# The opening of a delta-rule and MoE kernel: three written-out stages replaced by one order from a list scheduler inside the kernel

## The chip, the cores and the metric

One NeuronCore of a Trainium2 chip runs the whole program. The metric is the device time of one execution in microseconds; the median of the runs is quoted. Engines are named as in the profile: PE is TensorE's matmul, PEld its weight load, DVE is VectorE, ACT is ScalarE, POOL is GpSimd, SP is SyncE (here it only issues DMAs).

## What is computed

Three layers, one behind the other, on 4 x 768 = 3072 tokens:

```python
# 1: delta rule, 4 x 8 heads, 768 steps, head size 48
y_t = q_t @ state;  state += beta_t * outer(kn_t, v_t - kn_t @ state)    # kn = k / (|k| + 1e-6)
# 2: 384 -> 1024 -> 1024 -> 384, with a product of two projections
x = (((x @ w1) * (x @ w2)) @ w3) @ w_out
# 3: softmax-weighted hidden layer, layer norm, projection
h = x @ w_in;  solu = h * softmax(h)
out = ((solu - mean) / sqrt(var + 1e-6) * g_ln) @ w_out2
```

Layer 2's weights arrive as 8-byte floats and are converted in the kernel; w3 @ w_out is multiplied once, so that layer 2 needs w1, w2 and one product matrix.

## The kernel before

**The delta rule by chunks.** The 768 steps of each of the four batches are cut into chunks of 64. Chunks of two batches alternate, so the code handles *pairs* of chunks c, c+1. Eight chunks (four pairs) make a *set*; there are six sets. A set needs these steps:

- `load(i)`, `norm(i)`: four times per set, k and q are loaded by SP as 128 tokens and k is normalised (Square and Sqrt on ACT, four DVE operations). `norm` then issues four SP DMAs of 48 KB that copy the normalised k into the ring `kst` (lines 259 to 262).
- `prep_t(i)` (transposes on PE, copies into `KQ` and the ring `QA`) and `prep_g(i)` (products of keys and queries, four ACT copies, four masked DVE multiplications for each chunk).
- `invert(n)`, `invert_end(n)`: the triangular inverse of a whole set on DVE, 31 steps of two dependent operations (lines 342 and 348), two transposes before and after.
- `merge_1`, `merge_2`, `merge_3` for each pair: three rounds of small matmuls with copies in between, giving `TW`.
- `chain_u`, `chain_s`, `chain_y` for each pair, in sequence over all pairs: u from the state, the state's update, and the output y. y is written as two parts (`xb`) for layer 2.

**Layer 2** is `moe_block(j)`, twelve blocks of 256 tokens. A block is 14 portions: eight of 18 matmuls each (`pab`, line 591, with gate operations on ACT and DVE), then six of 12 (`px`, line 615). Its first reader of y is `pab`.

**The weights.** `weights_first` lists 18 pieces: four of w_out, eight of w3, three of w1, three of w2. `convert` turns a piece's 8-byte numbers into float32 in units of 384 or 512 columns: a low part (DVE, line 140), a high part (ACT Prelu, line 143), a shift (DVE, 150), an addition (DVE, 187). The w3 pieces are transposed on PE, copied on ACT (559), and multiplied with w_out (line 564); w1 and w2 are split into two parts (226 on ACT, 227 on DVE). The pieces of w_out and w3 are loaded by one DMA each, those of w1 and w2 by four for groups of 48, 48, 16 and 16 rows. They use seven slots, so a load waits until a slot's former piece has been used.

**The order of the work.** Before the main loop the program issues: four loads, set 0's `norm`, `prep_t`, `prep_g` with conversion steps put between them by `conv(x)` (a counter that lets some steps of the generator go), `invert(0)` with half a conversion step per operation, `invert_end(0)`. Then a loop over s = 0 to 23, a pair c = 2s each: `chain_u`, merges of the pairs to come, eight `turn`s, `chain_s`, `chain_y`. In the first two steps of a set the next set's `prep_t` and `prep_g` are done and its inverse is started; a `turn` also calls `fill(x)`, which lets x portions of layer 2 go. Block 0 may start when y of six chunks is there (`moe_all`, LAG = 2, line 759), and the conversion must be drained when c reaches 6 (line 802). PE's order is pinned to the program's order from line 796 on; the other engines' orders are the framework's.

Of the kernel before, what the change touches and what calls it, by code (L numbers as in the profile page):

```python
# [20 lines left out]
def kernel(  # L21
# [15 lines left out]
    nc = tc.nc  # L37
# [20 lines left out]
    CD = 6  # L58
    LAG = 2
# [3 lines left out]
    P0, C0 = 4, 24  # L63
    EX = 2.0
    F1 = (0.58, 0.6, 0.66, 0.66)
    LO = 2
    Z0, Z1 = 24, 44
# [66 lines left out]


# [99 lines left out]

    def load(i):
        b, s0 = chunk_at(chunk_of(i))
        for src, dst in ((k, kt_of(i)), (q, qt_of(i))):
            t = src[b].rearrange("(p e) s d -> s p e d", e=2)
            nc.sync.dma_start(  # L240
                out=dst.rearrange("t p (e x) -> t p e x", e=2)[:, :, :, 0:D], in_=t[s0:s0 + 128]
            )

    def norm(i):
        kt = kt_of(i).rearrange("t p (e x) -> t p e x", e=2)[:, :, :, 0:D]
        sq = small(NP * 2 * D).rearrange("t (p e d) -> t p e d", e=2, d=D)
        ss = pr.tile([128, NP, 2], F32, name="ss")
        rn = pr.tile([128, NP, 2, 1], F32, name="rn")
        nc.scalar.activation(out=sq, in_=kt, func=AF.Square)
        nc.vector.tensor_reduce(out=ss, in_=sq, axis=AX.X, op=ALU.add)  # L250
        nc.scalar.activation(out=ss, in_=ss, func=AF.Sqrt)
        nc.vector.tensor_scalar(out=ss, in0=ss, scalar1=1e-6, scalar2=None, op0=ALU.add)
        nc.vector.reciprocal(out=rn[:, :, :, 0], in_=ss)
        nc.vector.tensor_tensor(out=kt, in0=kt, in1=rn.to_broadcast([128, NP, 2, D]), op=ALU.mult)
        for cc in range(2):
            sl = (chunk_of(i) + 2 * cc) % RQ
            for h in range(2):
                o = 64 * (1 - h)
                nc.sync.dma_start(
                    out=kst[sl * 2 // RQ][64 * h:64 * h + 64, sl % (RQ // 2)],  # L260
                    in_=kt_of(i)[64 * cc:64 * cc + 64, :, o:o + D],
                )
# [4 lines left out]
    def prep_t(i):  # L267
        pk = ps_prep.tile([128, NP, 128], F32, tag="prep", name="pk")
        for p in range(NP):
            nc.tensor.transpose(pk[:, p, :], kt_of(i)[:, p, :], ident)  # L270
        nc.scalar.copy(out=KQ[0:KA, :, :, 1, :], in_=pk[0:KA].rearrange("r p (g t) -> r p g t", t=HC))
        pq = ps_prep.tile([128, NP, 128], F32, tag="prep", name="pq")
        for p in range(NP):
            nc.tensor.transpose(pq[:, p, :], qt_of(i)[:, p, :], ident)
        r = pq.rearrange("r p (c t) -> r c p t", c=2)
        (nc.vector.tensor_copy if i < SETC else nc.scalar.copy)(  # L276
            out=KQ[0:KA, :, :, 0, :], in_=pq[0:KA].rearrange("r p (g t) -> r p g t", t=HC)
        )
        sl = chunk_of(i) % RQ
        qa, sl = qa_of(sl)  # L280
        nc.scalar.copy(out=qa[0:64, sl:sl + 3:2, :, 1, :], in_=r[0:64])
        held[0] = nc.scalar.copy(out=qa[64:KA, sl:sl + 3:2, :, 0, :], in_=r[64:KA])
        if i < 2:
            load(i + 4)
        if i > 3 and i + 2 < NT128:
            load(i + 2)

    def prep_g(i):
        for cc in range(2):
            c = chunk_of(i) + 2 * cc  # L290
            (qa, sl), u0 = qa_of(c % RQ), c % SETC * NP
            pg = ps_prep.tile([128, NP, 128], F32, tag="prep", name="pg")
            for p in range(NP):
                for g in range(2):
                    for h in range(2):
                        r = slice(64 * (1 - h), 64 * (1 - h) + D)
                        o, x = 64 * h + HC * g, slice(HC * g, HC * g + 3 * HC)
                        nc.tensor.matmul(  # L298
                            pg[o:o + HC, p, x], KQ[r, p, 2 * cc + g, 1, :],
                            KQ[r, p, 2 * cc:2 * cc + 2].rearrange("r g k t -> r (g k t)")[:, x],  # L300
                            start=True, stop=True, skip_group_check=True,
                        )
            gd = GD[:, u0:u0 + NP, :]
            nc.scalar.copy(out=gd[:, :, :], in_=pg[:, :, HC:C])
            nc.scalar.copy(out=G21[:, c % SETC], in_=pg[:, :, HC:C])
            nc.scalar.copy(out=gd[32:64], in_=pg[32:64, :, 3 * HC:128])
            held[0] = nc.scalar.copy(out=gd[96:128], in_=pg[96:128, :, 3 * HC:128])  # L307
            for h in range(2):
                for r, x, o in (
                    (slice(64 * h, 64 * h + 64), slice(HC, C), C), (slice(64 * h, 64 * h + HC), slice(0, HC), 0),  # L310
                ):
                    nc.vector.tensor_tensor(  # L312
                        out=qa[r, sl, :, h, x], in0=pg[r, :, o:o + HC],
                        in1=mask[r, x].unsqueeze(1).to_broadcast([r.stop - r.start, NP, HC]), op=ALU.mult,
                    )

    bl = pr.tile([128, NSET, HC], F32, name="bl")

    def load_beta():
        for b in range(B):  # L320
            nc.sync.dma_start(
                out=bd.rearrange("(o k b) p e g i -> o b (p e) k (g i)", k=CPB, b=2)[b // 2, b % 2],
                in_=beta[b].rearrange("h (k x) -> h k x", k=CPB),
            )
        t = bd.rearrange("(n c) p e g i -> e g (c p) n i", c=SETC)
        for h in range(2):
            for g in range(2):
                r = 64 * h + 32 * g
                nc.sync.dma_start(out=bl[r:r + 32], in_=t[1 - h, g])

    def invert(n):
        nc.vector.transpose(out=Lz, in_=GD.rearrange("p u j -> p j u"))
        nc.gpsimd.memset(Tt, 0.0)
        nc.scalar.copy(out=Tt.rearrange("p i c -> p (i c)")[:, 0:HC * HC:HC + 1], in_=bl[:, n, :])  # L334
        yield nc.vector.scalar_tensor_tensor(
            out=Lz, in0=Lz, scalar=-1.0, in1=bl[:, n, :].unsqueeze(1).to_broadcast([128, HC, HC]),
            op0=ALU.mult, op1=ALU.mult,
        )
        for j in range(HC - 1):
            m = HC - 1 - j  # L340
            t = tmp[:, 0:m * (j + 1)].rearrange("p (i c) -> p i c", c=j + 1)
            yield nc.vector.tensor_tensor(  # L342
                out=t,
# [3 lines left out]
            )  # L347
            yield nc.vector.tensor_tensor(  # L348
                out=Tt[:, j + 1:HC, 0:j + 1], in0=Tt[:, j + 1:HC, 0:j + 1], in1=t, op=ALU.add
            )  # L350

    def invert_end(n):
        nc.vector.transpose(out=Dt.rearrange("p u i -> p i u"), in_=Tt)
        nc.vector.transpose(
            out=D1n.rearrange("p u c -> p c u"), in_=Tt.rearrange("p i c -> p c i")
        )

    def vcopy(c):  # L360
        return nc.vector.tensor_copy if 2 <= c < CA else nc.scalar.copy

    def dcopy(c):
        return nc.scalar.copy if c < 2 else nc.vector.tensor_copy

    def xcopy(c, lim):
        return nc.scalar.copy if c < lim or c % SETC >= SETC // 2 else nc.vector.tensor_copy
# [3 lines left out]
    def merge_1(c):  # L371

        tw, u0 = c % RT, c % SETC * NP
        both = slice(tw, tw + 2)
        mt = ps_prep.tile([128, 2, 2, NP, HC], F32, tag="prep", name="pm")
        pm, pt = mt[:, 0], mt[:, 1]
        for cc in range(2):
            for p in range(NP):
                for h in range(2):
                    nc.tensor.matmul(  # L380
                        pm[64 * h:64 * h + 32, cc, p, :],
                        G21[64 * h + 32:64 * h + 64, c % SETC + cc, p, :],
                        Dt[64 * h + 32:64 * h + 64, u0 + NP * cc + p, :],
                        start=True, stop=True, skip_group_check=True,
                    )
        xp = at.tile([128, 2, NP, HC], F32, name="xp")
        nc.scalar.copy(out=xp[0:32], in_=pm[0:32])
        vcopy(c)(out=xp[64:96], in_=pm[64:96])
        d = Dt[:, u0:u0 + 2 * NP, :].rearrange("r (c p) i -> r c p i", c=2)
        for g in range(4):  # L390
            r = slice(32 * g, 32 * g + 32)
            o = HC * (g % 2)
            (nc.scalar.copy if g < 2 else dcopy(c))(out=TW[r, both, :, g // 2, o:o + HC], in_=d[r])
        mg_t[c] = (xp, pt)

    def merge_2(c):
        xp, pt = mg_t.pop(c)
# [630 lines left out]
```

## Time and profile before

| | us |
|---|---|
| median of three runs (lowest, highest) | 863.81 (858.72, 864.83) |
| the profiled execution's own time | 862.37 |
| its span (first to last instruction) | 860.6 |
| PE busy | 802.0 (93%) |
| DVE busy | 581.9 (68%) |
| ACT busy | 467.7 (54%) |
| first `pab` matmul (layer 2 begins) | 153.72 |
| first `ph` matmul of the long last stage (layer 3) | about 633 |

Times in the rows count from the start of the span. A busy time is the union of an engine's instructions in a stretch, so overlapping instructions count once. The granted clock (PEclk) is given as a share of 2.4 GHz: 1.00 is that, 0.50 is 1.2 GHz.

### The profile page before, as it was taken

To read this page: it belongs to the slowest core of one execution; us is meant where nothing else is said; L and a number is where in the kernel's file an instruction comes from. 1 tells how busy PE (TensorE), PEld (TensorE's weight loads), DVE (VectorE), ACT (ScalarE), POOL (GpSimd) and SP (SyncE) were. 2 spreads that over 40 slices of the span, in tenths; PEclk is the share of its full clock that TensorE was granted. 3 is DMA by queue.
4 is the path that set the end of the run, shared out by engine and by line. 5 is a ranking of instruction groups with operands and counts; after the bars stand their busy time and mean duration, and the time that the engine had idled before them with its cause. 6 is when DMAs were issued, how large, how long until landed. Compare 5 with 4: busy or idle time off the path is not lost.

```text
span 860.6 us, 24611 instructions
## 1 busy us (share of the span) xinstructions
PE 802.0 (93%) x10256; PEld 731.3 (85%) x10256; DVE 581.9 (68%) x1522; ACT 467.7 (54%) x1127; POOL 46.2 (5%) x98
## 2 busy tenths in 40 slices
PE   4499668999999999999999999999999999999998
PEld 3366467999889999999999999999979999999997
DVE  4889996985497569756975596467656555555553
ACT  4564478457736764586468644565444443443442
POOL 7010000000000000000000000000001010000000
PEclk9999858999999999999999999999999999999999
DMA  9999814041413331332142113143331221221200
GB/s 225 299 235 155 130 20 82 15 94 30 95 30 66 78 68 36 82 69 61 35 85 48 43 35 95 30 125 107 119 122 58 72 64 56 74 65 56 74 28 28
DMA packets 140576, 70.74 MB, mean 82 GB/s; under 512 B 107057, under 2 KB 130865, under 8 KB 138673
## 3 DMA queue, kind: packets, MB, share of 16 engines
q1 hardware_dynamic: 138688, 57.64, 29.7%
q0 software_dynamic: 1776, 11.54, 4.2%
q8 instruction: 81, 1.33, 0.7%
q14 instruction: 31, 0.25, 0.1%
HBM read 47.91 MB, written 14.25 MB: 72 GB/s over the span
## 4 chain that ended last, share of the span: by engine, by line
PE 47%; issue 23%; DVE 16%; ACT 7%; DMA 3%; POOL 2%; SPq 0%; POOLq 0%; ACTq 0%; DVEq 0%
PE pab L591 17%; PE px L615 8%; PE pg L298 4%; DVE GT L348 3%; DVE tmp L342 3%; PE wps L564 3%; PE pw L425 3%; PE pu L451 2%; PE py L494 2%; PE pst L476 2%; DVE QA L312 2%; PE pm L404 2%; PE ph L918 1%; POOL vr L948 1%; DMA st_o<-in_moe_w_out_dram 1%
## 5 line engine op out<-in xcount | busy, mean ns | idle before, releaser
L591 PE MATMUL pab<-xb,w1s 128*128 128x256 f32 x864 | 123.7, 288 | 4.8 <-DVE asg L599 3.4
L591 PE MATMUL pab<-xb,w2s 128*128 128x256 f32 x864 | 119.2, 283 | 0.0
L591 PEld LDWEIGHTS pab<-xb,w1s 128*128 128x128 f32 x864 | 109.8, 191 | 8.7 <-DVE asg L599 4.7
L615 PE MATMUL px<-gh,Ws 128*128 128x256 f32 x864 | 112.7, 287 | 1.2 <-ACT gh L600 1.1
L591 PEld LDWEIGHTS pab<-xb,w2s 128*128 128x128 f32 x864 | 110.6, 192 | 0.0
L615 PEld LDWEIGHTS px<-gh,Ws 128*128 128x128 f32 x864 | 105.7, 191 | 3.3 <-ACT gh L600 1.5
L971 PE MATMUL po<-w4s,ln 128*128 128x384 f32 x432 | 79.8, 338 | 0.0
L918 PE MATMUL ph<-wis,x 128*128 128x512 f32 x288 | 76.7, 401 | 0.0
L600 ACT CAST gh<-asg 128x256 fp32r<-128x256 f32 x96 | 38.9, 405 | 68.6 <-DVE asg L599 67.6
L971 PEld LDWEIGHTS po<-w4s,ln 128*128 128x128 f32 x432 | 76.1, 188 | 0.0
L934 ACT ACTIVATE e<-ph,nm 128x1024 f32<-128x1024 f32 x24 | 26.8, 1118 | 87.5 <-DVE nm L933 86.0
L599 DVE TENSOR_TENSOR asg<-pab,asg 128x256 f32<-128x256 f32 x96 | 40.3, 420 | 46.4 <-ACT asg L598 46.1
L312 DVE TENSOR_TENSOR QA<-pg,mask 64x128 f32<-64x128 f32 x192 | 46.5, 281 | 34.2 <-ACT GT L307 19.4
L342 DVE TENSOR_TENSOR tmp<-D1n,GT 128x31 f32<-128x31 f32 (+15 forms) x186 | 63.0, 339 | 4.4 <-ACT GT L334 0.2
L348 DVE TENSOR_TENSOR GT<-GT,tmp 128x31 f32<-128x31 f32 (+15 forms) x186 | 63.1, 339 | 3.4
L918 PEld LDWEIGHTS ph<-wis,x 128*128 128x128 f32 x288 | 52.4, 189 | 10.6 <-issue 0.2
L598 ACT COPY asg<-pab 128x256 f32<-128x256 f32 x96 | 35.5, 370 | 40.9 <-PE pab L591 38.7
L933 DVE TENSOR_REDUCE nm<-ph 128x1 f32<-128x1024 f32 x24 | 29.4, 1225 | 40.4 <-PE ph L918 40.4
L298 PE MATMUL pg<-KQ 48*32 48x96 f32 x1536 | 44.0, 267 | 8.4 <-DVE KQ L276 7.7
L935 DVE SCALAR_TENSOR_TENSOR hs<-ph,e 128x1024 f32<-128x1024 f32 x24 | 29.4, 1225 | 30.9 <-ACT e L934 30.9
L601 DVE TENSOR_TENSOR gh<-asg,gh 128x256 fp32r<-128x256 f32 x96 | 40.4, 421 | 13.4 <-ACT gh L600 12.9
L298 PEld LDWEIGHTS pg<-KQ 48*32 48x32 f32 x1536 | 37.1, 118 | 13.1 <-ACT raw_w2s L143 6.3
(158 smaller groups left out, 1355.5 us busy)
## 6 DMA issues: line engine op xcount, KB each, us to landing
x2d<-xs SPq DMA_DIRECT2D x36, 256.0 KB, 2.4
x<-x2d SPq DMA_DIRECT2D x24, 384.0 KB, 3.6
X<-in_v_dram SPq DMA_DIRECT2D x48, 96.0 KB, 3.1
out_dram<-ot SPq DMA_DIRECT2D x24, 192.0 KB, 1.9
ktok<-in_k_dram SPq DMA_DIRECT2D x22, 192.0 KB, 3.8
qtok<-in_q_dram SPq DMA_DIRECT2D x22, 192.0 KB, 3.5
kst<-ktok SPq DMA_DIRECT2D x88, 48.0 KB, 2.9
raw_w2s<-in_moe_w_dram POOLq DMA_DIRECT2D x4, 1024.0 KB, 7.0
```

Of the source, the lines that this page charges most:

```text
L298: nc.tensor.matmul(pg[o:o + HC, p, x], KQ[r, p, 2 * cc + g, 1, :], KQ[r, p, 2 * cc:2 * cc + 2].rearrange("r g k t -> r (g k t)")[:, x], st ...
L312: nc.vector.tensor_tensor(out=qa[r, sl, :, h, x], in0=pg[r, :, o:o + HC], in1=mask[r, x].unsqueeze(1).to_broadcast([r.stop - r.start, NP, ...
L342: yield nc.vector.tensor_tensor(out=t, in0=Lz[:, j, j + 1:HC].unsqueeze(2).to_broadcast([128, m, j + 1]), in1=Tt[:, j, 0:j + 1].unsqueeze( ...
L348: yield nc.vector.tensor_tensor(out=Tt[:, j + 1:HC, 0:j + 1], in0=Tt[:, j + 1:HC, 0:j + 1], in1=t, op=ALU.add)
L591: nc.tensor.matmul(pab[:, e, :], ws[m][:, a, fs], xb[:, b, m, :], start=(n == 0), stop=(n == 3 * NM - 1), skip_group_check=True,)
L598: nc.scalar.copy(out=asb, in_=pab[:, 0, :])
L599: nc.vector.tensor_tensor(out=g, in0=pab[:, 1, :], in1=asb, op=ALU.mult)
L600: nc.scalar.copy(out=gh[:, 0, f, :], in_=g)
L601: gated[0] = nc.vector.tensor_tensor(out=gh[:, 1, f, :], in0=g, in1=gh[:, 0, f, :].bitcast(F32), op=ALU.subtract)
L615: nc.tensor.matmul(px, Ws[:, a, f, js], gh[:, b, f, :], start=(n == 0), stop=(n == 3 * NF - 1),)
L918: nc.tensor.matmul(ph[:, gs], x2[:, m, a, :], wis[m][:, b, gs], start=(n == 0), stop=(n == 3 * NM - 1),)
L971: nc.tensor.matmul(po, ln[:, a, f, :], w4s[f][:, b, :], start=(n == 0), stop=(n == 3 * NF - 1),)
```

## The change

Everything up to the end of set 0 (its four pairs' chain), all conversions, and set 1's `norm`, `prep_t`, `prep_g` and `invert(1)` are now one stretch, whose order on *every* engine is fixed by a list scheduler that runs while the program is built. Each step is a generator that yields operations with an engine, a cost in microseconds and a time from which its inputs are there; `Weave.go` picks, engine by engine, the earliest operation, and among those within `SLACK` the one with the lowest priority number. Costs, `TAIL` (time until another engine sees a result) and DMA landings (`land`) are constants. Some operations may go to either of ACT and DVE. `moe_block` runs in the same stretch as the thread of least priority. The main loop now begins with set 1 (s = 4).

```diff
-    CD = 6
-    LAG = 2
-    P0, C0 = 4, 24
-    EX = 2.0
-    Z0, Z1 = 24, 44
+    LW = 11
...
+    TAIL = {"PE": 0.21, "ACT": 0.13, "DVE": 0.12, "POOL": 0.15, "SP": 0.0}
+    SLACK = {"PE": 0.3, "ACT": 0.1, "DVE": 0.05, "POOL": 0.0, "SP": 0.0}
+    BIAS = {"PE": 0.0, "ACT": 0.0, "DVE": 0.3, "POOL": 0.0, "SP": 0.0}
...
+                        e, cost, fn = min(th[2][1], key=lambda a: max(self.free[a[0]], th[2][2]) + a[1] + BIAS[a[0]])
+                        best.setdefault(e, []).append((max(self.free[e], th[2][2]), th[0], th, cost, fn))
...
+                    first = min(x[0] for x in c)
+                    p = min((x for x in c if x[0] <= first + SLACK[e]), key=lambda x: (x[1], x[0]))
...
+    def store(i):
...
+                t = yield on("ACT", lambda e, sl=sl, h=h, o=o, cc=cc: plain(
+                    e, kst[sl * 2 // RQ][64 * h:64 * h + 64, sl % (RQ // 2)],
+                    kt_of(i)[64 * cc:64 * cc + 64, :, o:o + D]), 0.28, 0.28, t - 0.1)
...
+        t = yield op("PE", 0.46, lambda: turned(pk, kt_of(i)), at_)
...
+            t = yield op("PE", 0.75, products, ready.get(i, 0.0))
...
+    def unit(raw, o, n, at_, value, use):
...
+        a = yield either(
+            ("DVE", 0.08 + n / 1920, lambda: nc.vector.tensor_scalar(
+                out=low, in0=w[:, :, 0], scalar1=2.0 ** -29, scalar2=None, op0=ALU.mult)),
+            ("ACT", 0.06 + n / 1000, lambda: nc.scalar.mul(out=low, in_=w[:, :, 0], mul=2.0 ** -29)), at_)
...
+            "q0": lambda: ring[:, 0:2 * DFF], "q1": lambda: ring[:, 2 * DFF:4 * DFF],
...
+        "o0:a0 w0:b2 o1:a1 w1:q0 o2:b0 o3:b1 w2:q1 w3:xb w4:a0 w5:a1 w6:b0 w7:b1 "
+        "u0:q0 v0:q1 v1:b2 u1:a0 u2:a1 v2:xb"
...
+            if i == 0:
+                yield ("wait", came[3])
...
+                    todo_ = [(d[:, o:o + n], src[:, o:o + n]) for o, n in cuts(w)]
...
     def moe_block(j):
+        yield ("wait", ab_done)
+        yield ("wait", xb_set[j])
...
+    def first_chain():
...
+            if c == CPT:
+                yield ("wait", ab_done)
...
+            yield from chain_y(c, t)
...
+    def second_prep():
+        yield ("wait", inverted[0])
+        for i in range(SETC // 2, SETC):
+            yield ("spawn", 3.9, norm(i))
+        for x in ("u0", "v0"):
+            yield ("wait", spent[x])
...
+        for i in range(SETC // 2, SETC):
+            yield from prep_t(i)
...
+            yield from prep_g(i)
...
+        yield from beside(invert(1), 40, third_keys)
+        yield from invert_end(1)
...
+    for i in range(SETC // 2):
+        WV.spawn(0.1 + 0.01 * i, norm(i))
+        WV.spawn(0.2 + 0.01 * i, first_prep(i))
+    WV.spawn(0.3, first_inverse())
+    WV.spawn(0.3, first_merges())
+    WV.spawn(0.2, first_chain())
+    WV.spawn(4.0, convert_first(items))
+    WV.spawn(3.8, second_prep())
+    moe_thread = WV.spawn(9.0, mg, False)
+    WV.go()
...
-        chain_s(c)
-        chain_y(c)
-        y_done[0] = c + 2
+        run(chain_y(c))
+        run(chain_s(c))
```

Single conversion units are spawned with priority 5.0 and up. In the pieces' list `o`, `w`, `u`, `v` are w_out, w3, w1, w2, and the second name is the slot: `q0` and `q1` lie in the half of the `QA` ring that set 1 writes later (hence the wait for u0 and v0). A w_out or w3 piece is loaded by two DMAs of half its columns or rows. For sets 0 and 1 `store` replaces the `kst` DMAs by copies on ACT or DVE. Beta's first copy moves from SP's to ACT's queue, and SP's reload of it stands ahead of loads 2 and 3. `ab_done` is set when all 18 pieces are converted; block 0 waits for it. In the main loop y is done ahead of the state's update, and in a set's first two steps a `turn` lets the portion of layer 2 go before its other job.

## Rows read from the trace of the kernel before

**Rows 1.** Busy time of each engine by stretch, granted clock, DMA share, GB/s

```profile
core 0: us, PE busy (x) PEld busy (x) DVE busy (x) ACT busy (x) POOL busy (x), PEclk, DMA share, GB/s
0.00:153.00 153.00, 109.52 (x1418) 80.55 (x1420) 123.19 (x316) 92.56 (x217) 22.41 (x44) 0.89 0.78 162
7.00:153.00 146.00, 109.52 (x1418) 80.55 (x1420) 122.63 (x315) 90.22 (x214) 16.39 (x26) 0.88 0.77 163
0.00:10.00 10.00, 0.04 (x1) 0.07 (x2) 1.97 (x5) 3.82 (x5) 8.96 (x21) 1.00 0.99 185
70.00:80.00 10.00, 9.92 (x46) 6.58 (x45) 9.93 (x30) 4.95 (x10) 0.97 (x2) 1.00 0.89 136
110.00:120.00 10.00, 7.09 (x132) 6.15 (x132) 8.79 (x18) 8.77 (x22) 0.00 (x0) 0.50 0.10 19
158.70:190.00 31.30, 31.13 (x352) 30.34 (x353) 30.20 (x84) 14.75 (x38) 0.00 (x0) 1.00 0.23 46
190.00:240.00 50.00, 46.67 (x985) 43.38 (x984) 26.15 (x72) 35.49 (x98) 0.95 (x1) 1.00 0.31 68
```

**Rows 2.** PE in order of time: start us, us, engine, line, operation

```profile
10.84 1.06 PE L274 MATMUL pq<-ident,qtok 128*128 128x128 f32 x4
12.87 2.78 PE L298 MATMUL pg<-KQ 48*32 48x96 f32 x64 [0.97 <-DVE KQ L276]
...
134.34 0.63 PE L274 MATMUL pq<-ident,qtok 128*128 128x128 f32 x4 [0.84 <-DVE QA L312]
...
146.30 1.52 PE L298 MATMUL pg<-KQ 48*32 48x96 f32 x64
...
152.69 1.10 PE L425 MATMUL pw<-TW,kst 64*48 64x64 f32 x32
153.72 1.33 PE L591 MATMUL pab<-xb,w1s 128*128 128x256 f32 x9
```

**Rows 3.** DVE in order of time: inverse, end of conversion

```profile
100.74 1.90 DVE L353 STREAM_TRANSPOSE Dt<-GT 128x1024 f32<-128x1024 f32 x1
102.50 1.93 DVE L354 STREAM_TRANSPOSE D1n<-GT 128x1024 f32<-128x1024 f32 x1
...
126.14 0.69 DVE L227 TENSOR_TENSOR w2s<-raw_xb,w2s 128x512 fp32r<-128x512 f32 x1
```

**Rows 4.** Groups of instructions by line, engine, operation and tile

```profile
L348 DVE TENSOR_TENSOR GT<-GT,tmp 128x31 f32<-128x31 f32 (+15 forms) x186 | 63.1, 339 | 3.4
L342 DVE TENSOR_TENSOR tmp<-D1n,GT 128x31 f32<-128x31 f32 (+15 forms) x186 | 63.0, 339 | 4.4 <-ACT GT L334 0.2
L393 ACT COPY TW<-Dt 32x256 f32<-32x256 f32 x50 | 20.1, 403 | 17.3 <-DVE Dt L353 15.0 <-PE pu L451 1.8
L393 DVE COPY TW<-Dt 32x256 f32<-32x256 f32 x46 | 13.2, 287 | 3.1 <-PE pu L451 2.3
L140 DVE TENSOR_SCALAR t<-raw_w2s 128x512 uint32<-128x512 uint32 (+1 forms) x18 | 7.1, 406 | 0.1
```

**Rows 5.** DMA issues: queue, count, KB each, median us to landing

```profile
kst<-ktok SPq DMA_DIRECT2D x88, 48.0 KB, 2.9
raw_w2s<-in_moe_w_dram POOLq DMA_DIRECT2D x4, 1024.0 KB, 7.0
raw_w2s<-in_moe_w_dram SPq DMA_DIRECT2D x6, 384.0 KB, 5.6
stage_a<-in_moe_w_dram SPq DMA_DIRECT2D x2, 128.0 KB, 8.3
```

**Rows 6.** DMA issue on SP's and POOL's queues in order of time

```profile
98.14 1.52 SPq L178 DMA_DIRECT2D stage_a<-in_moe_w_dram  x3
...
12.21 0.92 POOL L178 DMA_DIRECT2D stage_a<-in_moe_w_out_dram  x1
```

More of the change, by code (lines that the diff above doesn't have):

```diff
@@ L253, in norm @@
[L253 to L257, printed above, removed]
-                o = 64 * (1 - h)
[L259 to L262, printed above, removed]
+        ss = pr.tile([128, NP, 2], F32, name="ss", bufs=2)
@@ L279, in prep_t, with queries @@
         sl = chunk_of(i) % RQ
         qa, sl = qa_of(sl)
[L281 to L284, printed above, removed]
+        def queries():
+            for o, x in ((qa[0:64, sl:sl + 3:2, :, 1, :], r[0:64]), (qa[64:KA, sl:sl + 3:2, :, 0, :], r[64:KA])):
+                e = yield on("ACT", lambda e, o=o, x=x: plain(e, o, x), 0.48, 0.6, b)
+            yield ("put", PP, e)
+            yield ("set", used[i], e)
@@ L285, in prep_t, with reload @@
+        yield ("spawn", 2.0, queries())
+        ready[i] = max(a, b)
+        def reload():
+            yield ("wait", stored[i])
+            yield from load(i + 2)
         if i > 3 and i + 2 < NT128:
-            load(i + 2)
+            yield ("spawn", 3.0, reload())
+    ready = {}
+    prepared = [Event() for _ in range(NT128)]
     def prep_g(i):
+        left, parts = [], []
         for cc in range(2):
@@ L354, in invert_end @@
[L354 to L367, printed above, removed]
+        yield op("DVE", 1.9, lambda: nc.vector.transpose(out=Dt.rearrange("p u i -> p i u"), in_=Tt))
@@ new lines, in use @@
+                t = yield op("PE", 0.46, turn, t)
+                yield ("set", turned_at[f"w{m}", o], t)
+                half_ = (o // 512) % 2
+                yield ("get", turned[half_])
+                w3t = bufs[half_][m % 2]
+                t = yield either(
+                    ("ACT", 0.48, lambda: nc.scalar.copy(out=w3t[:, 0:nb], in_=pt[:, 0:nb])),
+                    ("DVE", 0.6, lambda: nc.vector.tensor_copy(out=w3t[:, 0:nb], in_=pt[:, 0:nb])), t)
+                yield ("put", AB, t)
@@ new lines, in fill, with first_loads @@
+    def fill(x):
+        owed[0] = min(owed[0] + x, 3.0)
+        while owed[0] >= 1.0:
+            if not portion():
+                return
+            owed[0] -= 1.0
+    gated = [None]
+    head = tc.manual_schedule(engines=None)
+    head.__enter__()
+    warm = const.tile([128, 1], F32, name="warm")
+    nc.vector.memset(warm, 1.0)
+    nc.scalar.activation(out=warm, in_=warm, func=AF.Sqrt)
+    WV = Weave()
+    items = pieces()
+    def first_loads():
+        for i in (0, 1):
+            yield from load(i)
+        yield ("spawn", 4.0, fetch(items))
+        yield from load_beta_back()
+        for i in (2, 3):
+            yield from load(i)
+        for c in range(0, RX, 2):
+            yield from load_v(c)
+        yield op("SP", 0.6, lambda: nc.sync.dma_start(out=gl, in_=g_ln.rearrange("(k p) -> p k", p=128)))
+        for i in (4, 5):
+            yield ("wait", sent[NAMES[LW], 512])
+            yield ("wait", used[i - 4])
+            yield ("wait", stored[i - 4])
+            yield from load(i)
@@ L896 @@
     load_x2(1)
-    for x in mg:
+    while not over[0]:
+        portion()
         for _ in range(WO):
```

1041 lines of the change are left out of this document (717 added, 324 removed).

## The prediction

> **What bounds the kernel now.** I read the busy times by stretch first. From 158.7 us on PE is full (31.13 of 31.30 us), and in 190 to 240 it idles 3.3 us [rows 1]: layer 2 and the sets that follow are bound by PE. Ahead of that, no engine is full all the time: up to 153.0 DVE is busy 123.2 us, ACT 92.6 and PE 109.5, part of it at half clock (0.50 in 110 to 120) [rows 1]. Then PE in order of time: layer 2's first `pab` starts at 153.72, right behind a merge's `pw` [rows 2]. The work that PE has left at that moment fixes the end, since PE is full from there. So the question is when block 0 can start with the same work behind it.
>
> DVE in order of time tells why it is 153.72. Set 0's inverse ends with its two transposes at 100.74 and 102.50, and the last conversion (the split of w2's last unit) ends at 126.8 [rows 3]. From 104 to 153 the program issues merges, three pairs' chain and set 1's preparation in one written order, and in that stretch neither DVE nor ACT is full (8.79 and 8.77 of 10 in 110 to 120) [rows 1]. The early part is dense on DVE only (9.93 of 10 in 70 to 80, while ACT has 4.95) [rows 1]. So the stage is limited by DVE first and by latencies afterwards, and the two vector engines together have room: 215.8 us of work in 2 x 153.
>
> **The change part by part.**
>
> *Start of block 0.* In the changed code block 0 waits for y of the first two pairs and for `ab_done`, the conversion of all 18 pieces. Set 0's steps have the highest priorities, so its y is early; `ab_done` comes last, because single units have priority 5.0 and set 1's preparation 3.8. What must be done by then is nearly what the kernel before has done by 153: all conversions, sets 0 and 1 prepared, set 0's merges and most of its chain.
>
> *The sum of the two vector engines.* Before: 123.2 + 92.6 = 215.8 us [rows 1]. Added: `store` puts 2 sets x 4 x 4 = 32 copies on ACT or DVE in place of DMAs. The nearest rows are the copies of 32 x 256 elements, 0.287 us on DVE and 0.403 on ACT [rows 4], so 9.2 to 12.9 us; I take 11. (The DMA that goes took 2.9 us to land [rows 5]; it delays merges only, so I count nothing for its going.) Added also: that part of set 1's inverse that gets done ahead of the last unit. Its 62 operations take 0.339 us each, 21 us, with transposes some 26 [rows 4, 3]. They have the better priority, but an operation that depends on the one before is ready 0.12 - 0.03 = 0.09 us after that one's end in the scheduler's terms, beyond DVE's `SLACK` of 0.05; so where a unit's operation is ready it goes in between, and the two alternate. Once u0 and v0 are used, four pieces (8 units, 24 to 32 DVE operations) are left, and part of them go beside set 1's `prep`. I take 24 inverse operations ahead of the last unit, 8 us; the ends are 0 and 22. Sum 215.8 + 11 + 8 = 234.8.
>
> *How it is shared.* The low part (34 units, 0.406 us on DVE [rows 4]), the `KQ` copies, the transposed w3, `store` and the later halves of merges and chain may now go to either engine, and `BIAS` leans them to ACT. That is over 40 us that can be moved, more than the 31 us by which DVE led. So I take halves, 117.4 us each.
>
> *How full they get.* From 7.0, where norm(0) is about to finish, to 153 DVE was busy 122.6 of 146 us, 84% [rows 1]. In its dense stretch it was 99% [rows 1]. A fixed order made from constants will be worse than that and, with two chains of work and the conversions to choose from, better than 84%; I take 90%. Block 0 then starts at 7 + 117.4 / 0.90 = 137.4 us, 16.3 ahead of 153.72. The ends: 7 + (215.8 + 9.2) / 2 / 0.99 = 120.6 (33 us ahead), and 7 + (215.8 + 12.9 + 22) / 2 / 0.84 = 156.2 (2.5 late).
>
> *Work that moves behind block 0's start.* `chain_y(4)` waits for `ab_done` (its `xb` buffer holds w2's last piece), so one group of 32 matmuls, as long as the `pw` of 1.10 us [rows 2], moves behind: -1.1. What is left of inverse(1) runs beside `pab`, as it does before (DVE 30.20 of 31.30 with PE full [rows 1]): nothing. If that cover is gone, merges of set 1 are late, but two blocks' portions can fill PE there.
>
> *Queues.* SP: set 0's loads 2 and 3 now stand behind the reload of beta, which waits for beta's first copy; and POOL's weight loads wait for load 3, where the kernel before sent its second weight DMA at 12.21 and one from SP before that [rows 6]. I estimate weights 4 to 7 us later at the start, from nearby DMAs' landing times of 2.9 to 8.3 us [rows 5]. That hurts only while DVE waits for units in its first 20 us; it is in the 90%. At the other end nine slots stand in place of seven, so loads are issued earlier: before, the last ones were issued at 98.14 and landed 8.3 us later [rows 5, 6], far ahead of 137. Loads 4 to 7 of set 1 lie on SP behind waits for set 0's use of the buffers; who waits is set 1's norm, which has lower priority anyway.
>
> *Main loop.* y ahead of the state's update: the state's copies are read by the next pair's `chain_u`, four turns later, so I count 0. The swap inside a turn likewise. Both ends are 3 us, since all PE idles in 190 to 240 is 3.3 us [rows 1].
>
> Sum: 16.3 - 1.1 = 15.2 us. The profiled execution took 862.4 us (span 860.6 and 1.8 around it), 1.4 under the median of the runs; 862.4 - 15.2 = **847 us**.
>
> **The rivals.**
>
> *Better packing (832).* If units go first in practice and inverse(1) falls wholly behind, and the engines are nearly full, block 0 starts at 122. For it: DVE did hold 99% in a dense stretch. Against: set 0's preparation is a sequence of short dependent steps, and in 0 to 10 DVE has 1.97 us of work [rows 1].
>
> *Nothing gained (862).* All of inverse(1) gets ahead of the last units and the engines stay at 84%: block 0 at 154 to 156. The conversions before were done at 126.8; the change puts 26 us of set 1's inverse and its preparation in front of the last ones. What the early set 1 is worth would then be nothing, since PE was full beside inverse(1) already. Against it: the alternation worked out above.
>
> *Slower: PE's prices (881).* The scheduler prices four transposes at 0.46 us and a chunk's products at 0.75. Rows show 0.63 and 1.52 for two chunks at full clock, but 1.06 and 2.78 early on [rows 2], and a clock of 0.50 in 110 to 120 [rows 1]. Every engine's order is written as if results came at the cheap price. A DVE or ACT that has to wait for a late product holds back the conversion units queued behind it, though they are ready. Price: each `prep` is late by 2 x (1.06 - 0.46) + (2.78 - 1.50) = 2.5 us, eight of them 20 us; merges and chain of set 0, some 24 groups of matmuls at half clock, an estimated 0.6 each, 14 more. All 34 exposed would put block 0 at 171.4, and the end at 881. It is slower by over 1% once 24 of the 34 are exposed. Against: set 0's four `prep`s are late before as well, and then one or two engines wait at a time, with the other thread's work already queued ahead.
>
> *Halved weight loads (862).* A load of 1024 KB took 7.0 us to land, one of 384 KB 5.6, one of 128 KB 8.3 [rows 5]: time to land does not shrink with size. The change cuts 12 pieces into 24 DMAs. If two halves land one after the other, a piece takes about 11 in place of 7 us; over the eight w3 pieces 34 us, which moves the last landing from 106 to 140 and `ab_done` to about 153. In favour of it stands a rule; against it that both halves are issued at once and may overlap, and that a unit now waits for its half alone. The Trainium skill (DMA: Bandwidth & Descriptors, Rules for kernel authors) advises 128 partitions and at least 1 MiB for one DMA; by its fixed cost of about 2 us a DMA, 12 more would be an estimated 24 us if nothing overlapped. By that rule the change costs, by the rows it need not.
>
> **How the numbers follow.** Forecast 0.55 (its own range 838 to 858), better packing 0.13, nothing gained 0.17, halved loads 0.03, PE's prices 0.12. A measurement here tells about 1%, 8.6 us. Of the forecast's share 0.06 lies above 855. Faster: 0.49 + 0.13 = 0.62. Within 1%: 0.06 + 0.17 + 0.03 = 0.26. Slower: 0.12. The range reaches from 829 (a little beyond better packing, the low end's 33 us being 829) to 868, where part of the slow case is left out.
>
> **What would show it.** Right: first `pab` at 130 to 145; DVE and ACT busy shares in 20 to 130 both near 90%; low-part operations on ACT; about a third of inverse(1)'s operations ahead of the last split of w2; first `ph` earlier by as much as the first `pab`. Wrong: the last split of w2 near 150 with inverse(1) finished (nothing gained); DVE or ACT idle behind PE products with units queued (PE's prices); DVE idle behind weight DMAs beyond 40 us (halved loads); or a first `pab` that is early while PE idles afterwards by more than the 3.3 us of 190 to 240, in which case the gain is given back in the main loop.

## The result, and the profile after

| us | before | after |
|---|---|---|
| median (lowest, highest), four runs each | 862.31 (858.72, 864.83) | 848.05 (845.62, 848.62) |
| profiled execution, its span | 862.37, 860.6 | 848.23, 846.5 |
| block 0 of layer 2 runs without gaps from | 153.72 | 139.66 |
| `invert(1)`'s first closing transpose begins | 183.97 | 173.12 |
| first merge of set 1 (`pm`) | 187.24 | 175.30 |
| portions of layer 2 done by then | 15 | 16 |
| first `ph` (last stage) | 633.05 | 617.76 |

The ratio is 0.9839, with an interval of 0.982 to 0.9858: faster by 1.6%, 14 us. The forecast was 847.

Two rows of the kernel before belong to this table, the closing transpose on DVE and set 1's first merge on PE (columns of [rows 2]):

```profile
183.97 2.07 DVE L353 STREAM_TRANSPOSE Dt<-GT 128x1024 f32<-128x1024 f32 x1
187.24 0.69 PE L380 MATMUL pm<-Dt,G 32*32 32x32 f32 x32
```

Busy times by stretch of the changed kernel (us in the stretch, then busy us and instructions of PE, PEld, DVE, ACT and POOL, granted clock, DMA share, GB/s), in the columns of [rows 1]:

```profile
core 0: us, PE busy (x) PEld busy (x) DVE busy (x) ACT busy (x) POOL busy (x), PEclk, DMA share, GB/s
7.00:139.60 132.60, 101.54 (x1480) 71.45 (x1480) 110.93 (x303) 114.58 (x261) 24.73 (x42) 0.94 0.67 169
132.00:139.60 7.60, 2.64 (x42) 1.98 (x38) 7.53 (x17) 4.62 (x12) 0.96 (x1) 0.92 0.30 61
139.60:176.00 36.40, 35.83 (x349) 35.23 (x349) 33.64 (x96) 14.43 (x35) 0.00 (x0) 0.92 0.24 59
190.00:240.00 50.00, 48.54 (x1003) 45.56 (x1000) 34.54 (x101) 34.73 (x97) 0.96 (x1) 1.00 0.28 64
140.00:150.00 10.00, 10.00 (x111) 9.62 (x110) 8.31 (x25) 4.93 (x12) 0.00 (x0) 0.74 0.17 34
240.00:600.00 360.00, 352.71 (x5891) 339.02 (x5891) 245.24 (x674) 214.17 (x564) 3.69 (x5) 1.00 0.26 68
...
90.00:132.00 42.00, 36.58 (x925) 28.91 (x924) 30.84 (x88) 40.28 (x103) 2.30 (x2) 1.00 0.27 52
```

The work is now spread: in place of 122.6 us on DVE and 90.2 on ACT [rows 1], 110.9 and 114.6 us in 132.6, 84% and 86% full. Late in the stretch ACT is the fullest engine (40.28 of 42.00 in 90 to 132). From 139.60 on PE is full, as it was from 153.72.

PE in order of time of the changed kernel (start, us, engine, line, operation, idle time before and what ended it), in the columns of [rows 2]. Line 897 is w3 times w_out, 1023 is `pab`, 1065 `px`, 602 the first merge:

```profile
123.50 1.46 PE L897 MATMUL wps<-area,w3x 128*128 128x384 f32 x4
...
132.91 0.62 PE L1023 MATMUL pab<-xb,w1s 128*128 128x256 f32 x3
133.72 0.50 PE L1023 MATMUL pab<-xb,w1s 128*128 128x256 f32 x2 [0.20 <-ACT w1s L829]
136.78 0.61 PE L1023 MATMUL pab<-xb,w1s 128*128 128x256 f32 x3 [2.56 <-DVE w1s L830]
139.66 0.58 PE L1023 MATMUL pab<-xb,w1s 128*128 128x256 f32 x1 [2.26 <-DVE w1s L830]
140.04 2.12 PE L1023 MATMUL pab<-xb,w2s 128*128 128x256 f32 x9
...
147.66 1.24 PE L1023 MATMUL pab<-xb,w2s 128*128 128x256 f32 x9
...
175.30 0.69 PE L602 MATMUL pm<-Dt,G 32*32 32x32 f32 x32 [0.51 <-DVE Dt L558]
```

The first `pab` stands at 132.91, but it goes in small pieces until 139.66: it waits for the last splits of w1. Nine matmuls then take 2.12 us in place of 1.24. In 132 to 139.6 PE had been busy 2.64 of 7.60 us. In 140 to 150 the granted clock is 0.74, a mean of its levels 1.2 and 2.4 GHz: from 139.6 to 145 it is 0.50. The last line is the one that counts later: set 1's first merge waits 0.51 us for `invert(1)`'s transpose.

ACT in order of time (same columns) shows why those splits were late:

```profile
132.09 0.53 ACT L572 COPY GT<-pg 32x128 f32<-32x128 f32 x2
132.64 0.52 ACT L369 ACTIVATE t<-ktok 128x384 f32<-128x384 f32 x1
133.07 1.64 ACT L829 CAST w1s<-stage_a 128x512 fp32r<-128x512 f32 x3
```

These splits (line 829) have to wait for w3's last product, which PE ended at 125, because w1's buffers hold operands of that product. On ACT they then stand behind set 1's `prep` copies, until 133.07. And DVE, over the end of the conversion:

```profile
134.13 1.95 DVE L529 STREAM_TRANSPOSE D1n<-GT 128x1024 f32<-128x1024 f32 x1
...
136.06 0.67 DVE L830 TENSOR_TENSOR w1s<-stage_a,w1s 128x512 fp32r<-128x512 f32 x1
...
137.80 1.21 DVE L538 SCALAR_TENSOR_TENSOR D1n<-D1n,bl 128x1024 f32<-128x1024 f32 x1
138.93 0.67 DVE L830 TENSOR_TENSOR w1s<-stage_a,w1s 128x512 fp32r<-128x512 f32 x1
139.53 0.17 DVE L547 TENSOR_TENSOR tmp<-D1n,GT 128x31 f32<-128x31 f32 x1
...
173.12 2.04 DVE L558 STREAM_TRANSPOSE Dt<-GT 128x1024 f32<-128x1024 f32 x1
```

Of `invert(1)` only the preparation (lines 529 and 538) comes ahead of block 0, and each of the two operations stands in front of a split (line 830) that PE waits for. Its 62 operations run from 139.53 on, beside PE's portions. Its closing transpose begins 10.85 us earlier than before.

PE's waits in 120 to 720 (engine, line, what it waited for: us in all, times, longest):

```profile
PE pab L1023 <- DVE w1s L830: 4.8, 2, 2.6
...
PE pm L602 <- DVE Dt L558: 1.9, 2, 1.3
...
PE pab L1023 <- DMA xb<-xb: 0.9, 2, 0.5
```

The last line is to be remembered: in the main loop layer 2 hardly ever waits for its input `xb` (0.9 us in all; 1.3 in the kernel before). In the next section this wait grows to 31 us.

### The profile page after: what moved, and what is told of

It reads as the page before. It is cut to its first block, busy times and chain, and to the rows that moved or that the text cites. A ratio compares the mean times of both kernels' runs of the same rounds, so it can differ in the third digit from the quotient of the medians.

```text
span 846.5 us, 24616 instructions
## 1 busy us (share of the span) xinstructions
PE 792.9 (94%) x10256; PEld 723.1 (85%) x10256; DVE 571.5 (68%) x1511; ACT 490.0 (58%) x1172; POOL 53.6 (6%) x113
## 4 chain that ended last, share of the span: by engine, by line
PE 36%; issue 25%; DVE 23%; ACT 9%; DMA 4%; POOL 2%; SPq 0%; ACTq 0%; POOLq 0%; DVEq 0%
PE pab L1023 14%; DVE GT L553 6%; DVE tmp L547 6%; PE px L1065 5%; PE pg L465 3%; DVE asg L1036 2%; PE wps L897 2%; DVE gh L1042 2%; DMA stage_i<-in_moe_w_in_dram 2%; PE pw L671 2%; PE ph L1472 1%; POOL vr L1502 1%; PE pm L643 1%; PE pu L709 1%; PE py L769 1%
## 5 line engine op out<-in xcount | busy, mean ns | idle before, releaser
L1023 PE MATMUL pab<-xb,w1s 128*128 128x256 f32 x864 | 126.8, 292 | 9.4 <-DVE w1s L830 4.8
L1023 PEld LDWEIGHTS pab<-xb,w1s 128*128 128x128 f32 x864 | 111.7, 194 | 14.1 <-DVE w1s L830 5.2
L1065 PE MATMUL px<-gh,Ws 128*128 128x256 f32 x864 | 114.8, 288 | 0.1
L493 DVE TENSOR_TENSOR QA<-pg,mask 64x128 f32<-64x128 f32 (+1 forms) x192 | 47.0, 281 | 29.0 <-ACT GT L572 17.3
L465 PE MATMUL pg<-KQ 48*32 48x96 f32 x1536 | 39.4, 250 | 5.8 <-ACT KQ L427 4.5
L326 DVE TENSOR_TENSOR ln<-pt,ln 128x512 fp32r<-128x512 f32 x48 | 32.9, 690 | 16.2 <-ACT ln L325 13.6
```

The costliest lines, as they stand in the source:

```text
L465: nc.tensor.matmul(pg[o:o + HC, p, x], KQ[r, p, 2 * cc + g, 1, :], KQ[r, p, 2 * cc:2 * cc + 2].rearrange("r g k t -> r (g k t)")[:, x], st ...
L493: e = yield op("DVE", 0.21, lambda r=r, h=h, n_=n_, x=x, o=o: nc.vector.tensor_tensor(out=qa[r, sl, :, h, x], in0=pg[r, :, o:o + HC], in1= ...
L1023: nc.tensor.matmul(pab[:, e, :], ws[m][:, a, fs], xb[:, b, m, :], start=(n == 0), stop=(n == 3 * NM - 1), skip_group_check=True,)
L1065: nc.tensor.matmul(px, Ws[:, a, f, js], gh[:, b, f, :], start=(f == 0 and z == 0), stop=(f == NF - 1 and z == 2),)
```

## The experiments

All ratios are to the kernel before, with the interval in brackets; its median was 861.8 to 862.3 us each time, so the times of different runs can be compared. "Portions" are the ones of layer 2 that PE had done when set 1's first merge began, counted from the matmuls of lines 1023 (18 to a portion) and 1065 (12).

**1. Set 1 last.** The changed kernel with set 1's preparation behind the conversions:

```diff
-            yield ("spawn", 3.9, norm(i))
+            yield ("spawn", 6.1, norm(i))
...
-    WV.spawn(3.8, second_prep())
+    WV.spawn(6.0, second_prep())
```

> Changed kernel, but set 1's preparation and inverse get a worse priority than the conversion units (6.0 and 6.1 in place of 3.8 and 3.9). Theory A (the end is fixed by when layer 2's first block runs without stops, 139.7 us in the changed kernel, less the PE work moved behind that point): w3's last products no longer stand behind set 1's preparation, so the splits of w1 that wait for them come earlier; first uninterrupted pab at 118 to 127, set 1's preparation (10 us of PE) moves behind it, net gain 3 to 10 us: 838 to 845. Theory B (the gain comes from having set 1 ready early): set 1 is entered later and PE runs dry there, 852 to 860.

Measured: 891.61 us (888.81 to 895.12), ratio 1.0353 (1.0314 to 1.0393), slower than both kernels. Block 0 did begin earlier, at 127.97 without gaps, 11.7 us ahead of the changed kernel. All expectations missed. PE's waits in 120 to 720, and its busy times in 240 to 600 (columns as above):

```profile
PE pab L1023 <- DMA xb<-xb: 16.6, 17, 3.6
```

```profile
240.00:600.00 360.00, 334.45 (x5528) 315.71 (x5527) 223.80 (x607) 195.48 (x513) 3.70 (x5) 0.95 0.23 57
```

Layer 2 now waits for its input, 17 times, and in 240 to 600 PE is busy 334.45 us at a mean granted clock of 0.95, against 352.71 and 1.00. With its early block 0 this kernel loses 43.6 us to the changed one, most of it long after block 0: PE's 18 us less of busy time and an estimated 0.05 x 360 = 18 us by the clock, in that stretch. So "the earlier block 0, the better" is wrong. Two things differ when set 1 is entered: the time of its first merge, 186.02 in place of 175.30, and the number of portions done, 25 in place of 16.

**2. No lean to ACT.** The changed kernel with

```diff
-    BIAS = {"PE": 0.0, "ACT": 0.0, "DVE": 0.3, "POOL": 0.0, "SP": 0.0}
+    BIAS = {"PE": 0.0, "ACT": 0.0, "DVE": 0.0, "POOL": 0.0, "SP": 0.0}
```

> Changed kernel with the scheduler's lean away from DVE taken out (0.3 us to 0). Theory A1 (ACT, 96% busy in 90 to 132 while DVE has 73%, is what the conversions wait for there): work goes to DVE, block 0 starts 3 to 5 us earlier, 843 to 846. Theory A2 (the order of dependent steps on PE limits that stretch, not ACT's load): the start stays within 1.5 us, 847 to 850. If DVE becomes the bound in 25 to 90, where it is fuller: 850 to 854.

Measured: 875.12 (874.63 to 880.31), ratio 1.0166 (1.0133 to 1.0199). All expectations missed again: block 0 begins later (146.00), set 1's first merge stands at 187.40 with 18 portions done, and the wait for `xb` is back:

```profile
PE pab L1023 <- DMA xb<-xb: 12.1, 17, 2.3
```

**3. Layer 2 not woven in.** Sixteen portions (as many as the changed kernel has done at set 1's entry) stand in a row behind the stretch:

```diff
-    moe_thread = WV.spawn(9.0, mg, False)
+    moe_thread = None
...
+    for _ in range(16):
+        portion()
```

> Changed kernel with layer 2 taken out of the scheduled stretch: its first 16 portions stand in a row behind it. Theory A: PE waits for set 1's inverse with nothing to do, from about 133 to 165, and the 16 portions come afterwards: 20 to 32 us longer, 868 to 880, slower than the kernel before too. Theory C (the gain is that of a denser preparation, whatever stands beside the inverse): 848 to 853.

Measured: 849.84 (848.01 to 852.46), ratio 0.9861 (0.9834 to 0.9889). The interval overlaps the changed kernel's (0.982 to 0.9858), so putting layer 2's first blocks under the scheduler, one of the change's named parts, is worth nothing that shows here. `invert(1)` runs on DVE beside the row of portions anyway (its closing transpose begins at 174.93).

**4. The kernel before with LAG 0.** There block 0 has to wait for y of one pair more than it reads (LAG = 2 chunks); without that:

```diff
-    LAG = 2
+    LAG = 0
```

> Kernel before with one constant changed: block 0 may start when y of four chunks is there, not six. Theory A (what counts is the start less the work moved behind it): block 0 starts some 8 us earlier, but the third pair's chain, about 5 us of PE, moves behind it: 858 to 861. Theory D (the kernel before lost its time at this wait, conversions being done at 126.8): 849 to 854, most of the change's gain for one constant.

Measured: 933.83 (931.11 to 934.46), ratio 1.0827 (1.0803 to 1.0851). Both expectations missed. Without the hold the kernel before loses 72 us: 21 portions at set 1's entry, which is itself late (213.11), and 31.1 us of waits for `xb`:

```profile
PE pab L591 <- DMA xb<-xb: 31.1, 30, 4.9
```

What the first two runs showed is no trait of the new order.

**5. Four portions more.** This forms the theory that the expectations call L, the *stock*. Set 0's y feeds two blocks, 28 portions. From set 2 on a set's turns take 8 x (0.68 + 0.72 + 0.80 + 0.78) + 3 x 1.4 = 28.0 portions, and a set's y gives 28. So what was not taken by set 1's entry stays in stock for the whole run: 13 in the kernel before, 12 in the changed one, 10 in run 2, 3 in run 1 (and 3.8 more in each from set 2 on, since set 1's turns take 24.2). Where it is small, `pab` stands directly behind the y that it reads. By the constants 1.4 x 3 + 8 x 0.68 + 4 x 0.72 = 12.5 portions are let go from a set's entry to the y that its first block reads; the changed kernel comes into set 2 with 15.8, run 2 with 13.8, run 5 with 11.8, and what is over has to cover y's way into `xb`. This account by the constants is an estimate; it was not tried for itself. The test does the work of run 3 in another order, with 20 portions ahead of set 1 in place of 16:

```diff
-    for _ in range(16):
+    for _ in range(20):
```

> As e4, with 20 portions of layer 2 in a row behind the scheduled stretch in place of 16: the same work, four portions earlier. Theory L (the stock: a set's turns take 28 portions and its y supplies 28, so portions taken ahead of set 1 are missing in every later set, and layer 2 then waits for y just made): 856 to 875. Theory A (only what PE has left at the start counts): as e4, 848 to 853.

Measured: 891.45 (890.13 to 893.65), ratio 1.0342 (1.0316 to 1.0368): 41.6 us more than run 3 for four portions (of 168) done earlier, more than expected, with the expected sign. Set 1's first merge comes 6.8 us later behind the four portions (186.80 in place of 180.01), far less than that. First PE's waits in 120 to 720, then its busy times in 200 to 600, the columns as above:

```profile
PE pab L1023 <- DMA xb<-xb: 17.4, 18, 3.5
```

```profile
200.00:600.00 400.00, 369.65 (x6286) 347.40 (x6278) 253.07 (x694) 224.89 (x595) 4.65 (x6) 0.96 0.23 58
```

And run 3 in the same stretch:

```profile
200.00:600.00 400.00, 392.49 (x6750) 376.36 (x6749) 275.95 (x760) 242.98 (x642) 4.65 (x6) 1.00 0.27 69
```

PE is busy 22.8 us less. Its granted clock is 0.96 in place of 1.00, by which an estimated 0.04 x 400 = 16 us of full-speed work is missing. Together that is 39 of the 45.4 us between the two spans (891.7 and 846.3). Over the whole spans the account closes: the same 10256 matmuls keep PE busy 815.2 us in place of 794.9 at a mean granted clock of 0.962 in place of 0.984, which is 20.3 us, and it idles 25.1 us more. So the waits count nearly twice: PE's idle time, and the time at the lower level between them.

That `pab` stands directly behind y can be read in order of time. Block 9 in run 5:

```profile
541.91 1.15 PE L769 MATMUL py<-QA,X 112*64 112x64 f32 x32
543.00 0.92 PE L742 MATMUL pst<-X,kst 64*48 64x48 f32 x32
543.85 3.13 PE L1065 MATMUL px<-gh,Ws 128*128 128x256 f32 x24
550.27 0.66 PE L1023 MATMUL pab<-xb,w1s 128*128 128x256 f32 x3 [3.29 <-DMA xb<-xb]
```

The same block in run 3:

```profile
508.63 1.15 PE L769 MATMUL py<-QA,X 112*64 112x64 f32 x32
...
518.50 1.69 PE L1065 MATMUL px<-gh,Ws 128*128 128x256 f32 x12
520.02 1.24 PE L1023 MATMUL pab<-xb,w1s 128*128 128x256 f32 x9
```

In run 3 it starts 10.2 us behind the end of y (`py`), after work that fills PE, and does not wait; in run 5 7.2 us behind it, 3.29 of them idle.

**6 and 7. Runs 1 and 2 with layer 2 stopped after 16 portions** until the stretch is over:

```diff
             yield ("portion",)
+            if (j, f) == (1, 1):
+                yield ("wait", go_on)
...
+    go_on.t = 0.0
     todo[0] = moe_thread[2]
```

> As e1 (set 1's preparation behind the conversions), but layer 2 stops after 16 portions until set 1 is entered; e1 had done 25. Theory L: most of e1's loss of 43 us goes, 840 to 856. Theory B (set 1 ready late is what cost e1 its time): 870 or more.

> As e2 (no lean away from DVE), with layer 2 stopped after 16 portions until set 1 is entered; e2 had done 18. Theory L: 847 to 857. Theory A3 (DVE as the bound costs e2 its 27 us): 868 or more.

Measured: 859.73 (856.83 to 861.14), ratio 0.9972 (0.9955 to 0.9988), and 855.25 (854.41 to 858.5), ratio 0.9916 (0.9891 to 0.9941). Of run 1's 43.6 us 31.9 come back (its time is 3.7 us above theory L's range), of run 2's 27.1 us 19.9 (within the range). The `xb` waits are down to 1.2 and 0.6 us. The rest of run 6 is in the main one wait, the first line of its waits in 120 to 720:

```profile
PE pm L602 <- DVE Dt L558: 18.6, 2, 17.2
...
PE pab L1024 <- DMA xb<-xb: 1.2, 1, 1.2
```

With its portions done, PE stands 17.2 us before set 1's first merge, until `invert(1)`'s transpose at 185.97 is done. This is what set 1's early preparation is worth: 859.73 - 848.05 = 11.7 us. Run 7's rest is of the same kind: its first merge stands at 186.26, behind a wait of 4.3 us for the same transpose.

**8. Set 1 last, and a slower set 1.** Run 1 with the turns of set 1 taking 11 portions in place of 20, so that the stock is built up again:

```diff
-    F1 = (0.58, 0.6, 0.66, 0.66)
+    F1 = (0.32, 0.33, 0.36, 0.36)
```

> As e1 (set 1's preparation behind the conversions, layer 2 not stopped, 25 portions at set 1's entry), but set 1's turns let 11 portions go in place of 20, so that the stock of unread y behind set 1 is that of the changed kernel. Theory L: e1's earlier start of block 0 (uninterrupted from 128.0, 11.7 us ahead of the changed kernel's 139.7) now shows, 836 to 848, the fastest version. Against it: with fewer portions in set 1 PE idles behind the chain's steps there, 849 to 862.

Measured: 861.94 (860.66 to 864.35), ratio 0.9996 (0.9981 to 1.0012). The stock from set 2 on is 3 + 28 - 15.2 = 15.8, as much as the changed kernel's 12 + 28 - 24.2; the `xb` waits are down to 2.1 us, and 29.7 of the 43.6 us come back. The fastest version, which theory L had forecast, it is not: set 1 has too few portions to fill PE, in 200 to 240:

```profile
200.00:240.00 40.00, 32.82 (x668) 29.20 (x667) 24.65 (x74) 26.18 (x74) 0.96 (x1) 0.83 0.28 57
```

PE idles 7.2 of 40 us there at a clock of 0.83. Portions are taken early or late, but they can't be won.

**9. The same for the kernel before with LAG 0**, F1 at (0.41, 0.42, 0.46, 0.46):

> Kernel before with block 0 after four chunks as e7, and set 1's turns cut from 20 to 14 portions, which takes back the six portions more that e7 had done at set 1's entry. Theory L: nearly all of e7's loss of 72 us goes, 855 to 868. If it was the waits ahead of set 1 that cost e7 its time (set 1 was entered at 213 in place of 187): 885 or more.

Measured: 884.19 (881.47 to 885.71), ratio 1.0237 (1.0199 to 1.0276). 50 of the 72 us come back, less than theory L expected; the time lies 0.8 us under the other expectation (885 or more), in which set 1's late entry is what costs. Set 1 is entered at 210.70 in place of 187.24, 23.5 us late, and that is as much as the loss that stays, some 22 us. By this run 4's loss has two parts, the stock and the late entry.

**10. State ahead of y again**, in the main loop of the changed kernel:

```diff
-        run(chain_y(c))
         run(chain_s(c))
+        run(chain_y(c))
```

> Changed kernel with the main loop's order of before: the state's update ahead of y. By the prediction nothing, 847 to 850. Theory L allows some loss, since y and so the next block's input come about 1 us later for each pair, which counts where layer 2 waits for them: 849 to 856.

Measured: 850.98 (850.3 to 852.06), ratio 0.9871 (0.9849 to 0.9893), against 0.9839 (0.982 to 0.9858). Some 3 us for y first, with intervals that just overlap.

**11. Dearer prices for PE.** Run 3 with the prices of set 0's and 1's preparation near the longer of the measured rows:

```diff
-        t = yield op("PE", 0.46, lambda: turned(pk, kt_of(i)), at_)
+        t = yield op("PE", 1.05, lambda: turned(pk, kt_of(i)), at_)
...
-            t = yield op("PE", 0.75, products, ready.get(i, 0.0))
+            t = yield op("PE", 1.39, products, ready.get(i, 0.0))
```

> As e4 (16 portions in a row behind the scheduled stretch, so the stock is fixed), with PE's work in prep priced as at half clock, 1.05 us for four transposes and 1.39 for a chunk's products in place of 0.46 and 0.75. If the written orders lose time to the cheap prices, the stretch gets shorter: 840 to 846. By my reading (few waits of PE's products for each other, 8 us in all ahead of block 0) nothing to speak of: 847 to 853. Dearer prices may also be the wrong ones past 40 us, where the clock is 1.00: up to 856.

Measured: 855.98 (850.4 to 857.97), ratio 0.9912 (0.988 to 0.9944), no better than run 3's 0.9861, rather worse. The profiled execution is the lowest of the six, 850.4; the trace can't tell why four others took 855.65 to 857.97 (at a mean granted clock of 0.968 to 0.972, where the two lowest have 0.984 and 0.982). In it block 0's first whole groups come at 131.68, 9.4 us ahead of run 3, but two portions later PE has to wait:

```profile
147.43 1.12 PE L413 MATMUL pk<-ident,ktok 128*128 128x128 f32 x4 [6.05 <-DVE ktok L376]
153.02 2.29 PE L1023 MATMUL pab<-xb,w1s 128*128 128x256 f32 x9 [3.62 <-DVE asg L1036]
```

Set 1's first merge is at 180.97 against 180.01: block 0's early start alone buys nothing here either.

**12. Whole weight loads.** Run 3 with one DMA for a w_out or w3 piece:

```diff
-                    todo_ = [(d[:, z * DM:z * DM + DM], src[:, z]) for z in range(2)]
+                    todo_ = [(d.rearrange("p (a d) -> p a d", a=2), src)]
...
-                    todo_ = [(d[:, o:o + n], src[:, o:o + n]) for o, n in cuts(w)]
+                    todo_ = [(d, src)]
```

> As e4, with each piece of w_out and w3 loaded by one DMA as before the change, not two halves. If halved loads cost time, as the rule of 1 MiB for a DMA has it: 840 to 847. By the rows (halves are issued together and overlap; a unit waits for its half alone): 848 to 853, a little slower if anything.

Measured: 852.03 (851.39 to 853.16), ratio 0.9876 (0.9852 to 0.9901), the same as run 3 within the intervals. The halves cost nothing.

**Read together.** The runs with 15 or 16 portions ahead of set 1, by the profiled executions. "Block 0" is the time from which its groups of nine no longer wait for w1 or w2; PE has a later wait of 3.0 us in runs 3 and 12, and of 17.2, 4.3 and 9.7 us in runs 6, 7 and 11:

| kernel | block 0 | closing transpose | set 1's first merge | span |
|---|---|---|---|---|
| changed | 139.66 | 173.12 | 175.30 | 846.5 |
| run 3 | 141.05 | 174.93 | 180.01 | 846.3 |
| run 6 | 131.98 | 185.97 | 188.02 | 857.9 |
| run 7 | 147.54 | 184.21 | 186.26 | 856.8 |
| run 10 | 139.87 | 173.16 | 175.33 | 850.2 |
| run 11 | 131.68 | 178.74 | 180.97 | 848.7 |
| run 12 | 139.62 | 173.37 | 178.45 | 850.7 |
| before (15 portions) | 153.72 | 183.97 | 187.24 | 860.6 |

The span follows the time at which set 1 goes on, 666 to 675 us ahead of the end, more closely than the start of block 0, 705 to 726 us ahead of it. Within those 9 us the table does not tell the runs apart: run 3 goes on 4.7 us later than the changed kernel and has the same span.

## Why the prediction was right, and where it was not

The time came out 1 us from the forecast, and block 0's start 2.3 us (139.66 against 137.4). The two vector engines did bound the opening, and sharing their work did bring block 0 forward. But one step is wrong as a rule and held here by luck, and two terms are off in opposite directions.

- **"The work that PE has left at that moment fixes the end, since PE is full from there."** This step failed. PE is full from block 0 on only because it draws on layer 2's stock, and what it draws early it lacks later: run 5, with the work of run 3 and block 0 hardly moved (139.55 in place of 141.05), takes 41.6 us longer. The prediction had even counted on this filling: "If that cover is gone, merges of set 1 are late, but two blocks' portions can fill PE there." Run 1 is that case, with 25 portions taken, and it is slower. The step gave the right number because two things held together. The stock stayed (16 portions taken, 15 before). And `invert(1)` came nearly as much earlier as block 0 did: set 1's first merge moved from 187.24 to 175.30, 11.9 us, with one portion more done, two groups of 1.24, 2.5 us. That is 14.4 by set 1's entry and 14.1 by block 0's start; the profiled executions differ by 14.1.
- **"What the early set 1 is worth would then be nothing"** (in "nothing gained"). Wrong: with the portions held at 16 it is worth 11.7 us (run 6). With the 2.9 us of y first (run 10) that makes 14.6, about the whole gain of 14.3; whether the two simply add was not tried.
- **The sum of the two engines: 234.8 forecast.** Measured to 139.6: 112.82 + 117.30 = 230.1. The store copies were 18 on ACT (0.349 each) and 14 on DVE (0.273), 10.1 us against 11. The term for `invert(1)`, 8 us, was mis-sized: 1.95 + 1.21, some 3.2, and none of its 62 operations. The alternation that I had worked out is there in the trace, but in `invert(0)`: from 79.47 to 81.10 its operations and those of a conversion unit take turns, and its last transpose begins at 83.14 where it had begun at 102.50 [rows 3]. `invert(1)` came too late for it: set 1's last `prep` copies stood on ACT until 132.6.
- **How full they get: 90% forecast.** 84% and 86%. The forecast divides a sum that counts from 0 by a stretch that begins at 7.00; in these terms it is 115.05 of 132.66 us, 87%, worth 4.8 us late. The smaller sum is worth 2.6 us early. The difference is the 2.3 us of block 0.
- **Halves, 117.4 each.** Near (112.8 and 117.3), but not even over time: from 90 to 132 ACT had 96% and DVE 73%, and the last splits waited there. The low part has 36 units, not 34 (18 in the row shown, 18 more in two other tiles); 27 of them went to ACT.
- **What PE loses at its restart** was not in the sum: three groups of nine at 2.12, 2.12 and 1.82 us in place of 1.24, together 2.3 us.
- **y first: 0 with ends of 3 us.** About 3, the end of the bound (run 10).
- **Weights later at the start: in the 90%.** The first one was issued at 14.52, before at 12.21 and one earlier [rows 6]. Nothing in the runs tells its cost apart.

The rivals. *Better packing* did not come: the engines had their gaps. *PE's prices* did not come (848 in place of 881), and dearer prices won nothing (run 11). *Halved loads* did not come either, by the rows and run 12. DMA issues of the changed kernel and of run 12 (queue, count, KB each, median us to landing):

```profile
raw_w2s<-in_moe_w_dram POOLq DMA_DIRECT2D x6, 512.0 KB, 5.6
raw_w2s<-in_moe_w_dram POOLq DMA_DIRECT2D x3, 1024.0 KB, 5.7
```

1024 KB took 7.0 us in the kernel before [rows 5] but 5.7 in run 12, so a half is not much sooner than a whole; but the two halves do overlap. Of two issued at 46.33 and 46.84 one landed after 4.3 us and the other after 5.0; run 12's whole load, issued at 46.31, took 5.0. The Trainium skill (DMA: Bandwidth & Descriptors, Rules for kernel authors) asks for at least 1 MiB a DMA where the most bandwidth is wanted. Here a unit waits only for its half, and 849.84 with halves against 852.03 with whole loads shows no loss. *Nothing gained* did not come in the kernel as it stands. But the forecast's own last warning, a first `pab` that is early while PE idles afterwards, is just what runs 1, 4 and 5 are; in run 2 PE idles likewise, without the early `pab`. A rival "the portions run too early" should have had a chance: the kernel before has LAG = 2, a constant that holds block 0 back, and run 4 shows that taking it away costs 72 us.

Not tried: the single effect of the copies in place of `kst`'s DMAs, of nine slots in place of seven, and of the swap inside a turn. Open: what makes run 11 slower; why run 1, with 25 portions taken, loses hardly more than run 5 with 20 (891.61 and 891.45); and the differences of up to 9 us in the table. No run was faster than the changed kernel.

## What to carry to other kernels

An engine that is full now may be full on credit: count what it draws from a stock that a later stage needs, and ask what binds when that is used up, here the inverse of the next set. When an opening is made shorter, compare the state in which it leaves the work to the main loop (items done, items in stock, and when the next set can go on), not only its time; taking four items too many out of 168 cost three times what this whole change won. In experiments on such an opening hold that count fixed, or each result mixes two effects.

## What the runs showed that was not expected

- The size of the loss by a small stock, and that it repeats itself in each set: 18 waits for `xb` of 3.5 us at most in run 5, no single one of which stands out.
- Where PE waits a little more, the rows show less clock as well. In 200 to 600 it was 0.96 with PE busy 92% of the time, and 1.00 with 98%. In 200 to 240 of run 8 it was 0.83 with 82%.
- PE at its restart: after 7.6 us in which it was busy 2.64, nine matmuls took 2.12 us (granted clock 0.50 from 139.6 to 145), and 1.24 from 147.66 on.
